# Converting the second layer's weight pieces behind the cosine passes of the first layer's second half

## The chip, the cores and the metric

One core of one Trainium2 chip runs the whole program in one launch. The metric is the device time of one execution in microseconds (us), less is better.

## The reference, cut to what matters

The program is an attention with a memory term, followed by two dense layers. Each layer has 2304 tokens, a model width of 512 and an inner width of 2048.

```python
def _moe_ref(x, w_in, w_out):
    h = x @ w_in
    g = h * np.cos(h)
    return g @ w_out

def _moe2_ref(x, w_in, w_out):
    h = x @ w_in
    sp = np.where(h > 20.0, h, np.log1p(np.exp(np.minimum(h, 20.0))))
    g = h * np.tanh(sp)
    return g @ w_out

x = attention(q, k, v, M_prev, z_prev, beta)     # 2304 x 512
return _moe2_ref(_moe_ref(x, w1_in, w1_out), w2_in, w2_out)
```

## The kernel before, in words

**Numbers.** The weights arrive in double precision, as pairs of 32-bit words. A *piece* is 128 x 512 such numbers (512 KB). It is loaded into one of two staging buffers `wst` (L123, issued by SP) and turned into single precision by five passes: POOL scales the high word (`L117`, written `wst<-wst`), ACT converts the low word (`L126`), DVE joins both with a shift (`L127`), takes the sign (`L128`) and puts it in (`L131`). Then the value is split into two float parts for the matrix engine: a high part `w` (`scaled("wh", ...)`, by ACT and POOL in turn, `L113` or `L117` written `w<-wst`) and the rest (`L161`, by DVE and POOL in turn). So pieces with an even number end on ACT and DVE, and those with an odd number on POOL twice. The last pass frees the staging buffer, into which the piece after the next is loaded.

**Layers.** Each layer's inner width is cut into two halves of 1024, and each half into four tiles of four pieces, so 16 pieces a half. `load_half` returns the tiles and a generator that converts one piece per step: `ga` and `gb` for the first layer's halves, `gc` and `gd` for the second layer's. The first layer's first half (`m1`) runs beside the attention, its second half (`m2`) after it over blocks of 512 tokens (four of them, and one of 256), and then comes the second layer (`m3`). While `m2` runs, `gc` converts the 16 pieces that `m3` begins with.

**One unit of m2.** A unit is 128 of the inner width for a block of 512 tokens. `first` computes `h` on PE (12 products, L429); `second` multiplies the split result `g` with the output weights into the sums `y` (12 products, L487). Units go in pairs: PE computes `h` of a pair, then `y` of the pair before. A pair of units needs, in this order, ACT `u<-h` twice (L376), DVE `u` twice (L377), one ACT sine over both units (L381), DVE's product with `h` twice (L384, here called the cosine product; it also frees the buffer of `h`), ACT `g<-u` twice (L113), and POOL `g<-u,g` twice (L401, the low part of `g`). The 36 units are 18 pairs, four pairs to a block of 512 tokens. At the end of a block `fin_full` adds `y` to a stored part sum (L518 loads it, L520 adds), splits it (ACT L521, POOL L524, four of each) and stores both parts (L522, L525). SP loads the next block's `x` (L474, four loads), of which two wait until the block's last `h` has been read.

**Order.** The program is recorded in the order of the code, and a scheduler then sets each engine's own order, which the engine follows strictly. `tc.issue_after(i)` is a rule for that scheduler alone: what is recorded inside it on the engine of `i` comes behind `i` on that engine. It adds no semaphore. `marks` and `last_sin` hold such instructions. Each engine's queue is in order, so an instruction that waits holds up all behind it, on SP's queue of transfers too.

Of the kernel before, what the change touches and what calls it, by code (L numbers as in the profile page):

```python
# [14 lines left out]
ALU = mybir.AluOpType  # L15
# [28 lines left out]
def attention_moe_moe_kernel(  # L44
# [14 lines left out]
    nc = tc.nc  # L59
# [84 lines left out]
    def load_half(pool, tagp, source, kind):  # L144
        tiles = []
        for tl in range(NTL):
            tiles.append([pool.tile([P, NC, SM // 2] if k < 2 else [P, 2, DM], F32R, tag=f"{tagp}{k}{tl}", bufs=1,
                                    name=f"{tagp}{k}{tl}") for k in range(4)])

        def gen():  # L150
            for tl in range(NTL):
                for n, t in enumerate(source(tl)):
                    k = n // 2 * 2
                    dH, dL = tiles[tl][k], tiles[tl][k + 1]
                    if k == 0:
                        c = 2 * n
                        dH, dL = (x[:, c:c + 2, :].rearrange("p c f -> p (c f)") for x in (dH, dL))
                    else:
                        dH, dL = (x[:, n - 2, :] for x in (dH, dL))
                    scaled("wh", dH, t)  # L160
                    turn_of(kind).tensor_tensor(dL, t, dH.bitcast(F32), ALU.subtract)  # L161
                    yield 0
        return tiles, gen()

    def from_double(win, wout, half):
        def f(tl):
            for src in weight_pieces(win, wout, half, tl):
                yield to_f32(src)
        return f

    def drain(g):
        for _ in g:
            pass
# [190 lines left out]
    last_sin = [None]  # L364
    marks = {}

    def elem_cos(cast):

        state = []

        def f(h, last):
            if not state:
                state.append(wk.tile([P, 2, SM], F32, tag="u", name="u", bufs=BUFS["u"]))
            u2 = state[0]
            u = u2[:, len(state) - 1]
            nc.scalar.activation(u.bitcast(I32), h, AF.Copy, scale=INV2PI, bias=0.25)  # L376
            nc.vector.scalar_tensor_tensor(u, u.bitcast(I32), -TWO_PI, h, ALU.mult, ALU.add)  # L377
            state.append(h)
            if len(state) < 3:
                return []  # L380
            last_sin[0] = nc.scalar.activation(u2, u2, AF.Sin, bias=c_hpi).ins  # L381
            out = []
            for i in range(2):
                nc.vector.tensor_tensor(u2[:, i], state[1 + i], u2[:, i], ALU.mult)  # L384
                out.append(split(u2[:, i], cast, "gl"))
            state.clear()
            return out
        return f
# [8 lines left out]
    def split(g, cast, kind):  # L397
        gg = wk.tile([P, 2, SM], F32R, tag="g", name="g", bufs=BUFS["g"])
        gH, gL = gg[:, 0], gg[:, 1]
        scaled(cast, gH, g)  # L400
        turn_of(kind).tensor_tensor(gL, g, gH.bitcast(F32), ALU.subtract)  # L401
        return gH, gL
# [191 lines left out]
    w_c, gc = load_half(w0p, "w2", from_double(w2i, w2o, 0), "w2l")  # L594
    m2 = ffn(b_pools, seq2, {1: w_b}, elem_cos("bh"), load_block(xsH, xsL, True), mm2_t, fin_full)
    with tc.issue_after(marks["sp"]):
        for i, _ in enumerate(m2):
            if i % 4 == 1:
                next(gc, None)
    drain(gc)  # L600
    w_d, gd = load_half(w1p, "w3", from_double(w2i, w2o, 1), "w3l")
    with tc.issue_after(last_sin[0]):
# [72 lines left out]
```

## Time and profile before

| what | value |
|---|---|
| three timed runs | 1094.81, 1095.95 and 1102.28 us, median 1095.95 us |
| the profiled execution, its own time | 1098.41 us |
| its span, first to last instruction | 1096.6 us |
| PE busy with products | 1056.2 us (96% of the span) |
| DVE, ACT, POOL busy | 517.7, 472.7, 428.4 us |
| mean granted clock of PE | 0.978 of full |

PE is TensorE, DVE VectorE, ACT ScalarE, POOL GpSimd, SP SyncE. The profile shows one execution, in us from the first instruction on. "Idle before it, ended by" names what an engine waited for last. What lies outside of the span (1098.41 less 1096.6) belongs to no instruction.

### The profile page before, as it was taken

To read this page: it belongs to the slowest core of one execution; us is meant where nothing else is said; L and a number is where in the kernel's file an instruction comes from. 1 tells how busy PE (TensorE), PEld (TensorE's weight loads), DVE (VectorE), ACT (ScalarE), POOL (GpSimd) and SP (SyncE) were. 2 spreads that over 40 slices of the span, in tenths; PEclk is the share of its full clock that TensorE was granted. 3 is DMA by queue.
4 is the path that set the end of the run, shared out by engine and by line. 5 is a ranking of instruction groups with operands and counts; after the bars stand their busy time and mean duration, and the time that the engine had idled before them with its cause. 6 is when DMAs were issued, how large, how long until landed. Compare 5 with 4: busy or idle time off the path is not lost.

```text
span 1096.6 us, 17569 instructions
## 1 busy us (share of the span) xinstructions
PE 1056.2 (96%) x6672; PEld 903.1 (82%) x6672; DVE 517.7 (47%) x1246; ACT 472.7 (43%) x947; POOL 428.4 (39%) x454
## 2 busy tenths in 40 slices
PE   6889899999999999999999999999999999999998
PEld 4767688888888899987777888988888888888897
DVE  7999885647474657655785232656200000000000
ACT  6776475637373633334454343543421222232231
POOL 5987563425242424455576333454211101010100
PEclk8998799999999999999999999999999999999999
DMA  6565442414131265333455432643300210110010
GB/s 214 184 193 189 141 145 66 140 59 138 60 95 35 80 221 182 122 114 125 165 200 183 144 116 77 218 139 97 129 6 1 77 39 0 58 39 1 20 39 20
DMA packets 66373, 117.04 MB, mean 107 GB/s; under 512 B 5616, under 2 KB 25072, under 8 KB 66288
## 3 DMA queue, kind: packets, MB, share of 16 engines
q1 hardware_dynamic: 66288, 115.91, 32.1%
q8 instruction: 53, 0.87, 0.3%
q14 instruction: 32, 0.26, 0.1%
HBM read 87.58 MB, written 28.31 MB: 106 GB/s over the span
## 4 chain that ended last, share of the span: by engine, by line
PE 70%; DVE 11%; DMA 7%; ACT 5%; POOL 4%; issue 3%; SPq 0%; ACTq 0%; POOLq 0%; DVEq 0%
PE h L429 29%; PE y L496 18%; PE y L487 12%; PE o L333 3%; PE tp L306 3%; PE sp L246 3%; DMA wst<-in_w1i_dram 2%; DVE wst L127 2%; DMA wst<-in_w1o_dram 2%; DVE wst L131 2%; DMA wst<-in_w2o_dram 1%; PE o L322 1%; DVE wst L128 1%; DMA wst<-in_w2i_dram 1%; DVE w L161 1%
## 5 line engine op out<-in xcount | busy, mean ns | idle before, releaser
L429 PE MATMUL h<-xbH,w 128*128 128x256 f32 (+1 forms) x1536 | 398.0, 340 | 8.0 <-DVE u L384 5.2
L429 PEld LDWEIGHTS h<-xbH,w 128*128 128x128 f32 x1536 | 268.1, 190 | 43.7 <-DVE u L384 6.9
L429 PE MATMUL h<-xbL,w 128*128 128x256 f32 (+1 forms) x768 | 259.3, 338 | 0.2 <-DMA xbL<-xsL 0.2
L487 PE MATMUL y<-g,w 128*128 128x256 f32 (+1 forms) x1344 | 224.8, 321 | 2.1 <-POOL g L401 1.2
L487 PEld LDWEIGHTS y<-g,w 128*128 128x128 f32 x1344 | 195.8, 195 | 24.3 <-issue 3.3
L496 PE MATMUL y<-w,g 128*128 128x512 f32 x864 | 201.8, 389 | 0.0
L496 PEld LDWEIGHTS y<-w,g 128*128 128x128 f32 x864 | 162.0, 188 | 33.4
L401 DVE TENSOR_TENSOR g<-e,g 128x512 fp32r<-128x512 f32 x36 | 25.3, 702 | 288.9 <-ACT g L113 258.3
L429 PEld LDWEIGHTS h<-xbL,w 128*128 128x128 f32 x768 | 146.1, 190 | 15.9 <-DMA xbL<-xsL 0.8
L401 POOL TENSOR_TENSOR g<-e,g 128x512 fp32r<-128x512 f32 x36 | 47.7, 1325 | 276.4 <-ACT g L113 276.4
L401 POOL TENSOR_TENSOR g<-u,g 128x512 fp32r<-128x512 f32 x72 | 95.9, 1347 | 122.0 <-ACT g L113 64.7
L274 POOL TENSOR_SCALAR at<-at,sm,omg 128x128 f32<-128x128 f32 (+2 forms) x144 | 108.4, 762 | 87.7 <-DVE sm L272 60.7
L393 ACT ACTIVATE e<-h 128x512 f32<-128x512 f32 x72 | 42.8, 594 | 216.6 <-PE h L429 216.2
L126 ACT ACTIVATE wst<-wst,c_seven 128x512 int32<-128x512 uint32 x64 | 49.3, 772 | 96.5 <-DMA wst<-in_w2o_dram 32.2
L127 DVE SCALAR_TENSOR_TENSOR wst<-wst 128x512 int32<-128x512 int32 x64 | 54.2, 847 | 68.1 <-POOL wst L117 34.4
L251 ACT ACTIVATE at<-at,mn 128x128 f32<-128x128 f32 (+3 forms) x128 | 71.0, 555 | 32.1 <-DVE mn L248 29.7
L377 DVE SCALAR_TENSOR_TENSOR u<-u,h 128x512 f32<-128x512 int32 x72 | 49.0, 682 | 61.7 <-ACT u L376 61.7
L376 ACT ACTIVATE u<-h 128x512 int32<-128x512 f32 x72 | 41.8, 591 | 80.9 <-PE h L429 72.3
L306 PE MATMUL tp<-ident,at 128*128 128x128 f32 x384 | 67.2, 294 | 8.0 <-DVE xL L338 3.1
L117 POOL TENSOR_SCALAR wst<-wst 128x512 f32<-128x512 f32 x64 | 46.9, 733 | 71.1 <-DMA wst<-in_w2o_dram 18.9
L333 PE MATMUL o<-aT,vt 128*64 128x128 f32 (+1 forms) x896 | 65.0, 276 | 0.0
L248 DVE CUSTOM_DVE_ANT_0 at<-sp,mask 128x128 f32<-128x128 f32 (+3 forms) x128 | 58.9, 481 | 10.7 <-PE sp L246 9.9
(94 smaller groups left out, 1244.9 us busy)
## 6 DMA issues: line engine op xcount, KB each, us to landing
wst<-in_w1i_dram SPq DMA_DIRECT2D x16, 512.0 KB, 3.8
wst<-in_w1o_dram SPq DMA_DIRECT2D x16, 512.0 KB, 4.1
wst<-in_w2i_dram SPq DMA_DIRECT2D x16, 512.0 KB, 3.7
wst<-in_w2o_dram SPq DMA_DIRECT2D x16, 512.0 KB, 3.6
qd<-in_qT_dram SPq DMA_DIRECT2D x16, 320.0 KB, 3.3
vt<-in_vn_dram SPq DMA_DIRECT2D x16, 320.0 KB, 3.3
xbH<-xsH SPq DMA_DIRECT2D x20, 256.0 KB, 4.7
xbL<-xsL SPq DMA_DIRECT2D x20, 256.0 KB, 4.7
```

Source lines behind the costliest of these rows:

```text
L126: nc.scalar.activation(lo, lo.bitcast(U32), AF.Relu, scale=-(2.0 ** -29), bias=c_seven)
L127: nc.vector.scalar_tensor_tensor(lo, hi, 3, lo, ALU.logical_shift_left, ALU.bitwise_or)
L248: nc.vector.tensor_tensor_reduce(at[:, :N], sp[:, :N], mask[:, SM - q0:SM - q0 + N], SSC, 3.0e38, ALU.add, ALU.min, mn[:, j:j + 1])
L251: marks["act"] = nc.scalar.activation(at[:, :N], at[:, :N], AF.Exp, bias=mn[:, j:j + 1], scale=-1.0, accum_out=sm[:, j:j + 1]).ins
L274: turn_of("sc", b == 0).tensor_scalar(at[:, :N], at[:, :N], sm[:, j:j + 1], gates[j], ALU.mult, ALU.mult)
L306: nc.tensor.transpose(tp[:, c:c + P], at[:, c:c + P], ident)
L333: marks["pe"] = nc.tensor.matmul(o[j * D:(j + 1) * D, :n], st["vt"][:kk, c, j * D:(j + 1) * D], a, start=False, stop=c == i, skip_group_ch ...
L377: nc.vector.scalar_tensor_tensor(u, u.bitcast(I32), -TWO_PI, h, ALU.mult, ALU.add)
L401: turn_of(kind).tensor_tensor(gL, g, gH.bitcast(F32), ALU.subtract)
L429: nc.tensor.matmul(h[:, a * T:(a + 1) * T], w_[:, c, f0:f0 + P], x_[c], start=m == 0, stop=m == 3 * NC - 1)
L487: nc.tensor.matmul(y[e // per][:, cols], w_[:, f, es], g_, start=fst and m == 0 and e % per == 0, stop=lst and m == 2, skip_group_check=True)
L496: nc.tensor.matmul(y[t], g_[:, tsl], w_[:, f, :], start=fst and m == 0, stop=lst and m == 2, skip_group_check=True)
```

## The change

The two cosine products of a pair are now remembered as `marks["cos"]` (the second of them stays), and each step of `gc` in `m2` is recorded inside two `issue_after` blocks: on DVE the piece's passes come behind the last cosine product recorded so far, on ACT behind the last sine recorded so far. A step of `gc` is still taken once per pair of units, right after the pair before has got its `second`; POOL and SP get no such rule.

```diff
@@ -381,7 +381,7 @@
             for i in range(2):
-                nc.vector.tensor_tensor(u2[:, i], state[1 + i], u2[:, i], ALU.mult)
+                marks["cos"] = nc.vector.tensor_tensor(u2[:, i], state[1 + i], u2[:, i], ALU.mult).ins
                 out.append(split(u2[:, i], cast, "gl"))
@@ -596,7 +596,8 @@
     with tc.issue_after(marks["sp"]):
         for i, _ in enumerate(m2):
             if i % 4 == 1:
-                next(gc, None)
+                with tc.issue_after(marks["cos"]), tc.issue_after(last_sin[0]):
+                    next(gc, None)
     drain(gc)
```

What that does to the order shows at three places. On ACT, at the second pair of `m2`, the order before was this (`wst` is a staging buffer, `w_6519` the high part of the third piece):

```order
L126 ACTIVATE wst<-wst,c_seven 128x512
L376 ACTIVATE u<-h 128x512
L126 ACTIVATE wst<-wst,c_seven 128x512
L376 ACTIVATE u<-h 128x512
L381 ACTIVATE u<-u,c_hpi 128x1024
L113 ACTIVATE w_6519<-wst 128x512
L113 ACTIVATE g<-u 128x512 x2
```

and now, for the second and the third pair, it is this:

```order
L376 ACTIVATE u<-h 128x512 x2
L381 ACTIVATE u<-u,c_hpi 128x1024
L126 ACTIVATE wst<-wst,c_seven 128x512
L113 ACTIVATE g<-u 128x512 x2
L376 ACTIVATE u<-h 128x512 x2
L381 ACTIVATE u<-u,c_hpi 128x1024
L126 ACTIVATE wst<-wst,c_seven 128x512
L113 ACTIVATE g<-u 128x512 x2
L113 ACTIVATE w_6519<-wst 128x512
```

Two conversions stood before the pair's sine, one of them between the two `u<-h`; now one stands behind each sine and none before it. DVE's passes moved in the same way, behind L384.

On POOL, about the end of the first block of `m2`, the order before was this:

```order
L401 TENSOR_TENSOR g<-u,g 128x512
L117 TENSOR_SCALAR wst<-wst 128x512
L401 TENSOR_TENSOR g<-u,g 128x512
L524 TENSOR_TENSOR yl<-yp,yh 128x512 x2
L117 TENSOR_SCALAR wst<-wst 128x512
L117 TENSOR_SCALAR w_6525<-wst 128x512
L161 TENSOR_TENSOR w_6526<-wst,w_6525 128x512
L524 TENSOR_TENSOR yl<-yp,yh 128x512 x2
```

and now it is this, from the pair ahead of the block's end to the pair behind it:

```order
L401 TENSOR_TENSOR g<-u,g 128x512 x2
L117 TENSOR_SCALAR w_6519<-wst 128x512
L161 TENSOR_TENSOR w_6520<-wst,w_6519 128x512
L117 TENSOR_SCALAR wst<-wst 128x512
L401 TENSOR_TENSOR g<-u,g 128x512 x2
L524 TENSOR_TENSOR yl<-yp,yh 128x512 x3
L117 TENSOR_SCALAR wst<-wst 128x512
L524 TENSOR_TENSOR yl<-yp,yh 128x512
L401 TENSOR_TENSOR g<-u,g 128x512 x2
```

One piece's first pass stands between each two pairs of L401; where it follows an L161, that L161 frees the very buffer into which its piece is loaded.

On SP, the loads of `x` for the third block of `m2` stood before behind four loads of pieces:

```order
L518 DMA yp<-ysP 128x512
L123 DMA wst<-in_w2i_dram 128x2x512 x2
L123 DMA wst<-in_w2o_dram 128x1024 x2
L474 DMA xbH<-xsH 128x2x512
L474 DMA xbL<-xsL 128x2x512 x2
L474 DMA xbH<-xsH 128x2x512
```

and now behind two:

```order
L525 DMA ysL<-yl 128x512
L123 DMA wst<-in_w2o_dram 128x1024
L123 DMA wst<-in_w2i_dram 128x2x512
L474 DMA xbL<-xsL 128x2x512
L474 DMA xbH<-xsH 128x2x512
L474 DMA xbL<-xsL 128x2x512
L474 DMA xbH<-xsH 128x2x512
L123 DMA wst<-in_w2i_dram 128x2x512
```

The last piece load ahead of `x` now takes the buffer of a piece of two pairs earlier. On PE nothing moves but six products of `y`, at one place.

## Rows read from the trace of the kernel before

**Rows 1.** Stages: length, busy PE, PEld, DVE, ACT, POOL, clock, DMA share, GB/s
```profile
520.00:540.00 20.00, 17.72 (x72) 14.17 (x71) 13.23 (x20) 9.23 (x15) 11.47 (x10) 0.91 0.59 209
...
620.00:640.00 20.00, 20.00 (x90) 16.56 (x89) 7.12 (x11) 8.23 (x12) 5.09 (x5) 1.00 0.26 91
```

**Rows 2.** Waits of PE's products, 470 to 800 us: total, times, longest, us
```profile
PE h L429 <- DVE u L384: 5.2, 4, 2.3
PE h L429 <- DMA xbH<-xsH: 2.0, 1, 2.0
```

**Rows 3.** Timeline of PE: start us, us, instruction, idle before it and releaser
```profile
507.66 0.39 PE L429 MATMUL h<-xbH,w 128*128 128x512 f32 x1
...
511.98 0.50 PE L429 MATMUL h<-xbH,w 128*128 128x512 f32 x1 [1.44 <-DVE u L384]
...
525.47 0.50 PE L429 MATMUL h<-xbH,w 128*128 128x512 f32 x1 [2.28 <-DVE u L384]
...
585.39 0.50 PE L429 MATMUL h<-xbH,w 128*128 128x512 f32 x1 [2.00 <-DMA xbH<-xsH]
...
595.14 0.39 PE L429 MATMUL h<-xbH,w 128*128 128x512 f32 x1
```

**Rows 4.** Timeline of ACT at the second pair
```profile
506.93 0.77 ACT L126 ACTIVATE wst<-wst,c_seven 128x512 int32<-128x512 uint32 x1 [2.10 <-DMA wst<-in_w2o_dram]
507.61 0.57 ACT L376 ACTIVATE u<-h 128x512 int32<-128x512 f32 x1
510.05 1.15 ACT L381 ACTIVATE u<-u,c_hpi 128x1024 f32<-128x1024 f32 x1 [1.87 <-DVE u L377]
```

**Rows 5.** Timeline of DVE at the second pair
```profile
509.33 0.68 DVE L377 SCALAR_TENSOR_TENSOR u<-u,h 128x512 f32<-128x512 int32 x1
...
511.23 1.29 DVE L384 TENSOR_TENSOR u<-h,u 128x512 f32<-128x512 f32 x2 [0.61 <-ACT u L381]
```

**Rows 6.** The chain that ended last, pieces in time: start us, us, what
```profile
611.62 5.44 PE y L487 x24
...
622.50 5.44 PE y L487 x24
...
694.20 4.79 PE h L429 x21
```

**Rows 7.** Timeline of ACT, a pair without conversions
```profile
613.01 1.15 ACT L381 ACTIVATE u<-u,c_hpi 128x1024 f32<-128x1024 f32 x1 [0.76 <-DVE u L377]
614.92 1.23 ACT L113 ACTIVATE g<-u 128x512 fp32r<-128x512 f32 x2 [0.76 <-DVE u L384]
```

**Rows 8.** Timeline of DVE, the same pair
```profile
614.20 1.29 DVE L384 TENSOR_TENSOR u<-h,u 128x512 f32<-128x512 f32 x2 [1.22 <-ACT u L381]
```

**Rows 9.** Timeline of POOL, the same pair, and a pass of a block's end
```profile
615.63 2.53 POOL L401 TENSOR_TENSOR g<-u,g 128x512 fp32r<-128x512 f32 x2 [5.14 <-ACT g L113]
...
639.95 1.31 POOL L524 TENSOR_TENSOR yl<-yp,yh 128x512 fp32r<-128x512 f32 x1
```

**Rows 10.** Tile wst, 500 to 600 us: ns min/median/max, first and last start
```profile
L117 POOL TENSOR_SCALAR wst<-wst x17: 638/650/1197, 503.7 to 596.6; 128x512 f32<-128x512 f32 x17
L126 ACT ACTIVATE wst<-wst,c_seven x15: 751/767/802, 503.6 to 584.2; 128x512 int32<-128x512 uint32 x15
L127 DVE SCALAR_TENSOR_TENSOR wst<-wst x15: 685/694/1679, 504.4 to 585.0; 128x512 int32<-128x512 int32 x15
L128 DVE TENSOR_SCALAR wst<-wst x15: 416/425/1514, 505.6 to 586.2; 128x512 int32<-128x512 int32 x15
L131 DVE TENSOR_TENSOR wst<-wst x15: 685/687/1672, 508.4 to 587.8; 128x512 int32<-128x512 int32 x15
...
L161 DVE TENSOR_TENSOR w<-wst,w x8: 674/684/1715, 500.2 to 585.6; 128x512 fp32r<-128x512 f32 x8
...
L161 POOL TENSOR_TENSOR w<-wst,w x8: 1291/1314/1761, 510.0 to 591.4; 128x512 fp32r<-128x512 f32 x8
...
DMA to landing us min/median/max: 3.5/3.7/5.9
```

## The prediction

> **What bounds the kernel now.** I read the table of stages first, then what PE waited for, then the timelines of the four engines about the waits. PE is the bound nearly everywhere: from 620 to 640 us it is busy for 20.00 of 20 us at full clock [rows 1]. In the second half of the first layer there is one stretch where it isn't, from 500 to 600 us, as in the stage from 520 to 540 us with 17.72 us at 0.91 of the clock [rows 1]. PE waits there four times for the cosine product L384 (5.2 us in all) and once for a load of x (2.0 us) [rows 2].
>
> The size of that loss is read from PE's own pitch. A pair of units, 24 products of h and 24 of y, takes 622.50 - 611.62 = 10.88 us where nothing disturbs [rows 6]. From the third pair's h at 507.66 us to the tenth's at 595.14 us there are seven pairs [rows 3]: 87.48 us, where 7 x 10.88 = 76.16 would do. So 11.3 us are lost there: the waits of rows 2 (7.2 us), short waits for g, the slow products after the longest wait (the stage mean of 0.91 is a stretch at the lower of the clock's two levels, 1.2 instead of 2.4 GHz, and it comes after the 2.28 us gap), and the slow start after each gap.
>
> Why the waits arise shows at the second pair. ACT stands at a piece's L126, waits 2.10 us for its load until 506.93 us, and only then runs the pair's second u<-h at 507.61 [rows 4]. On DVE the piece's passes come next, and the second L377 starts at 509.33, the cosine product at 511.23 [rows 5]; PE's second h of the third pair needs the buffer that this product frees and goes on at 511.98 us, 1.44 us late [rows 3]. So the chain of a pair is held up by piece passes that wait for transfers and stand ahead of it in the same queues. The load of x at 585.39 us is late for the same reason: SP issued it behind four piece loads, each of which waits for a staging buffer.
>
> **The change part by part.** No instruction is added or removed. The same 16 pieces are converted, one per pair instead of two or so, and behind the sine and the cosine product instead of ahead.
>
> *The chain of a pair.* Take T as the end of a pair's h, 611.62 us in the undisturbed pair [rows 6]. The sine runs from T+1.4 to T+2.5, L384 from T+2.6 to T+3.9, g from T+3.3, and L401 from T+4.0 to T+6.5 [rows 7 to 9]. The needs are later. The next pair's second h wants the first product of L384 (T+3.3) after y (5.44) and one h (2.72), at T+8.2: 4.9 us to spare. The pair's own y wants the first L401, 1.3 us long, at T+10.9: it may start as late as T+9.6, 5.6 us to spare. These margins now cover the passes of a piece.
>
> *ACT.* L126 (0.77) stands between the sine and g. The sine ends at T+2.5, so L126 ends at T+3.3, just when g could start anyway: cost nothing. If its cover (L384 on DVE) were gone, it would cost 0.77 us out of 5.6.
>
> *DVE.* L127, L128 and L131 (0.69 + 0.43 + 0.69 = 1.8 us) follow L384 and end at T+5.7; for an even piece ACT's high part (as long as L126, 0.77 at most) and L161 (0.68) follow until T+7.2 [rows 10]. The next L377 is due only after T+8.2. Cost nothing, by one us of cover.
>
> *POOL, where a wait is added.* Behind L401 an odd piece has its high part and L161, 0.65 + 1.31 us, until T+8.5. Only then is its buffer free; the load takes 3.7 us (median) to 5.9 (longest) [rows 10], so it is there at T+12.2 to T+14.4, and L117 ends at T+12.9 to T+15.1. The next pair's L401 is queued behind that L117 and is due at T+10.9+4.0 = T+14.9. So it is 0.2 us late at the most, with 5.6 us to spare behind it. I take nothing.
>
> *SP.* The last piece load ahead of x now waits for the buffer of an even piece, free at T+7.2 of its pair, while the x loads wait for the next pair's h to end, at T+10.9. The x wait of 2.0 us should go.
>
> *The end.* Piece 15 goes with the sixteenth pair. Counted on from the tenth pair at 595.14 us by 10.88 us, that pair's h ends at about 666 us, less what is saved, and its last pass some 9 us later. The second layer's first h comes at 694.20 us [rows 6]: nearly 20 us of cover, and none of its waits rest on the last pieces.
>
> *Passes that meet.* The same DVE passes range from 0.69 to 1.68 (L127), 0.43 to 1.51 (L128) and 0.69 to 1.67 us (L131) [rows 10]. The Trainium skill (SBUF — State Buffer, section Who interferes with whom) says that a DVE instruction with two SBUF inputs, or in a two-port mode, and a GpSimd instruction that reads SBUF take one shared port pair, and that the loser is blocked for the whole instruction. It speaks against this change, which sets the DVE passes right beside L401 in every pair; the long ends of the rows agree with it. By the medians the sum stays as it is; by that rule the time would be that of the first rival below.
>
> *Sum.* All of the 11.3 us may go; below nothing they can't be had again, since no other stall lies in this half. Bounds: 11.3 us gained, or, if the block ends keep a loss, down to 4 or 5 gained. I take 10.3, with 1.0 us left for three block ends at about 0.3 each, near the undisturbed end because the block ends that ran without pieces (after 620 us) show no wait of PE. The profiled execution would go from 1098.41 to 1088.1 us (its span from 1096.6 to 1086.3). The timed median, 1095.95, lies 2.5 us below the profiled time; the same gain puts it at 1085.7 us.
>
> **The rivals.** *Block ends keep a loss.* There four passes L524 (1.31 each) join POOL, and L117 of a piece stands between the third and the fourth, ahead of the next pair's L401. With the longest DVE passes everywhere, L384's end at T+3.9 plus 1.68 + 1.51 + 1.67 + 0.77 + 1.72 puts the buffer free at T+11.3, the load in at T+17.2, L117 and one L524 done at T+19.2 [rows 9, 10]; the next L401 must start by T+20.5. That is 1.3 us to spare, and a load held up by 3 us behind the stores of that block end would cost 1.7 us, three times: some 5 us, 1091 us. For it: the long rows, and four stores in the same queue. Against: by the medians 7.6 us are to spare.
>
> *Nothing moves in time.* The waits come from the block ends and the load of x rather than from queue order, and turn up elsewhere: about 1096 us. For it: half of the loss is not in the four L384 waits. Against: the pairs without pieces run at 10.88 us, block ends included.
>
> *The other side: POOL stands in front of its own load.* Each L117 waits for a load that can't start before the L161 ahead of it. T+8.5 + load + 0.65 passes T+20.5 from a load of 11.3 us on; from there each us of load is a us of PE in up to 14 pairs. At 12.1 us the gain is eaten; at 12.4 us 15 us are lost and the time is 1101 us; at 12.8 us it is over 1107. For it: x loads, part sums and stores share the transfer engines with the pieces. Against: the longest landing of 17 was 5.9 us, in a stretch with 209 GB/s [rows 1, 10].
>
> **How the numbers follow.** Chances: forecast 0.70, block ends 0.16, nothing 0.07, POOL 0.07. A measurement of this kernel tells about 1%, here 11.0 us, from no change, and the most that can be gained is 11.3. So the forecast itself lies at the border: I put 0.36 of its 0.70 beyond 1% and 0.34 within. With 0.16, 0.07 and 0.03 of POOL's within 1%, that is 0.60 the same; 0.04 slower. The range goes from 1083.5 (all 11.3 gained, and a run as far below the median as the fastest of the three, 1.1 us) to 1093.5 (the block ends at half as much again); it leaves out "nothing", POOL and a little below.
>
> **What would show it.** Right: PE at 20.00 of 20 us in all stages from about 500 us on, no wait of h for L384 over half a us, the tenth pair's h near 584 us, the clock at 1.00 throughout, the second layer's first h near 683 us, L126 spread over all of this half, about one per 10.88 us. Wrong in a step: waits of y for L401 (POOL's queue), of h for a load of x (SP's), or of h for L384 every fourth pair (block ends). The forecast is wrong as a whole if the seven pairs from the third to the tenth take more than 82 us, or if a loss of over 3 us comes up outside of them.

## The result and the profile after

| | before | after |
|---|---|---|
| timed runs, median | 1095.62 us of 4 (1094.81 to 1102.28) | 1084.97 us of 4 (1079.77 to 1091.44) |
| ratio, 95% interval | | 0.9891 [0.9861, 0.992] |
| profiled execution, its span | 1098.41, 1096.6 us | 1085.15, 1083.4 us |
| mean granted clock of PE | 0.978 | 0.987 |

The changed kernel is 1.1% faster: 10.65 us between the medians, where 10.3 was forecast (1085.7 us, measured 1084.97). The interval alone allows gains from 8.8 to 15.2 us, and the four timed runs of after lie up to 11.7 us apart, so that the medians came within 0.7 us of the forecast is partly luck; what follows rests on the traces.

A stage of after that answers to [rows 1] (length, busy PE, PEld, DVE, ACT, POOL, clock, DMA share, GB/s):

```profile
520.00:540.00 20.00, 20.00 (x90) 16.57 (x89) 12.06 (x16) 9.28 (x14) 9.51 (x10) 1.00 0.47 164
```

All stages from 500 to 760 us have PE at 20.00 of 20 us and a clock of 1.00. What PE's products waited for from 470 to 800 us in after (total, times, longest, us). The one line that is left is the end of the half before, and it stands in before too, with 0.9 us:

```profile
PE y L487 <- DVE g L115: 1.0, 1, 1.0
```

Both lines of [rows 2] are gone, and PE is full at full clock. The chain that ended last shows it as PE's pitch (start us, us, what):

```profile
505.88 5.44 PE h L429 x24
511.32 5.44 PE y L487 x24
...
582.03 5.44 PE h L429 x24
...
680.93 4.79 PE h L429 x21
```

From the third pair's h at 505.88 us to the tenth's at 582.03 are 76.15 us, 7 x 10.88, where before took 87.48 us [rows 3].

**Where the 13.2 us of span went.** To compare runs I read one stretch in each timeline of PE: from the last 46 products y of the half before to the first product of the second layer's y, L496. First before's two ends, then after's:

```profile
491.37 5.77 PE L487 MATMUL y<-g,w 128*128 128x256 f32 x46
...
710.73 4.47 PE L496 MATMUL y<-w,g 128*128 128x512 f32 x19
```

```profile
489.42 5.77 PE L487 MATMUL y<-g,w 128*128 128x256 f32 x46
...
697.46 4.70 PE L496 MATMUL y<-w,g 128*128 128x512 f32 x20
```

That is 219.36 us before and 208.04 after: 11.32 us, all that the prediction said could be had. Another 1.95 us lie ahead of the stretch, where the change does nothing; they can't be counted as its gain, since two runs below with one and the same order of instructions (cut256 and cut128) began the stretch 5.6 us apart, at 492.09 and 486.54 us. The expectations quoted below use a stretch inside this one, 33 us shorter (175.05 us in after, 186.54 in before); 33 is to be added to their numbers.

**A pair in after.** Take T as the end of its h, 511.32 us. First ACT and then DVE (start us, us, instruction, idle before it and its releaser):

```profile
512.71 1.15 ACT L381 ACTIVATE u<-u,c_hpi 128x1024 f32<-128x1024 f32 x1 [0.76 <-DVE u L377]
513.76 0.75 ACT L126 ACTIVATE wst<-wst,c_seven 128x512 int32<-128x512 uint32 x1
514.62 1.23 ACT L113 ACTIVATE g<-u 128x512 fp32r<-128x512 f32 x2
```

```profile
513.89 1.29 DVE L384 TENSOR_TENSOR u<-h,u 128x512 f32<-128x512 f32 x2 [1.22 <-ACT u L381]
515.10 0.68 DVE L127 SCALAR_TENSOR_TENSOR wst<-wst 128x512 int32<-128x512 int32 x1
...
518.17 0.97 DVE L161 TENSOR_TENSOR w<-wst,w 128x512 fp32r<-128x512 f32 x1 [0.74 <-ACT w L113]
```

L126 waits for nothing, where it waited 2.10 us in [rows 4], and the sine and the cosine product start at T+1.4 and T+2.6 as in a pair without a piece [rows 7, 8]. In before, ACT waited for 13 loads from 500 to 600 us (total, times, longest):

```profile
ACT wst L126 <- DMA wst<-in_w2o_dram: 14.9, 8, 3.7
ACT wst L126 <- DMA wst<-in_w2i_dram: 9.2, 5, 3.3
```

In after no L126 of these pieces waits for its load. POOL still does; its waits in after from 490 to 680 us:

```profile
POOL wst L117 <- DMA wst<-in_w2i_dram: 31.9, 8, 5.1
POOL wst L117 <- DMA wst<-in_w2o_dram: 23.6, 6, 5.2
```

So the waits for loads did not vanish. The 24.1 us on ACT are gone, and POOL's, 15.8 us in before's 500 to 600 us, are now 55.5; but POOL has them to spare, and none reaches PE.

### The profile page after: what moved, and what is told of

Same layout as the page of the kernel before. It is cut to its first block, busy times and chain, and to the rows that moved or that the text cites. A ratio compares the mean times of both kernels' runs of the same rounds, so it can differ in the third digit from the quotient of the medians.

```text
span 1083.4 us, 17564 instructions
## 1 busy us (share of the span) xinstructions
PE 1051.3 (97%) x6672; PEld 901.1 (83%) x6672; DVE 531.2 (49%) x1246; ACT 474.2 (44%) x947; POOL 434.3 (40%) x454
## 4 chain that ended last, share of the span: by engine, by line
PE 80%; DVE 7%; ACT 5%; DMA 4%; issue 2%; POOL 1%; SPq 0%; ACTq 0%; POOLq 0%; DVEq 0%
PE h L429 33%; PE y L496 18%; PE y L487 16%; PE o L333 3%; PE tp L306 3%; PE sp L246 3%; DMA wst<-in_w1i_dram 1%; DMA wst<-in_w1o_dram 1%; PE mp L286 1%; PE o L322 1%; DVE wst L131 1%; ACT at L251 1%; DVE wst L127 1%; DVE w L161 1%; DVE at L248 1%
## 5 line engine op out<-in xcount | busy, mean ns | idle before, releaser
L496 PE MATMUL y<-w,g 128*128 128x512 f32 x864 | 201.8, 389 | 0.0
L496 PEld LDWEIGHTS y<-w,g 128*128 128x128 f32 x864 | 161.9, 188 | 33.5
L401 DVE TENSOR_TENSOR g<-e,g 128x512 fp32r<-128x512 f32 x36 | 25.3, 702 | 288.9 <-ACT g L113 258.4
L401 POOL TENSOR_TENSOR g<-e,g 128x512 fp32r<-128x512 f32 x36 | 47.6, 1322 | 275.6 <-ACT g L113 275.6
L401 POOL TENSOR_TENSOR g<-u,g 128x512 fp32r<-128x512 f32 x72 | 102.3, 1438 | 70.7 <-DVE g L115 51.7
L117 POOL TENSOR_SCALAR wst<-wst 128x512 f32<-128x512 f32 x64 | 45.6, 713 | 116.7 <-DMA wst<-in_w2i_dram 40.6
L376 ACT ACTIVATE u<-h 128x512 int32<-128x512 f32 x72 | 42.3, 594 | 97.0 <-PE h L429 85.8
L126 ACT ACTIVATE wst<-wst,c_seven 128x512 int32<-128x512 uint32 x64 | 48.9, 766 | 68.6 <-DMA wst<-in_w1o_dram 19.6
L377 DVE SCALAR_TENSOR_TENSOR u<-u,h 128x512 f32<-128x512 int32 x72 | 49.0, 683 | 51.0 <-ACT u L376 50.8
L127 DVE SCALAR_TENSOR_TENSOR wst<-wst 128x512 int32<-128x512 int32 x64 | 50.0, 781 | 41.6 <-ACT wst L126 20.4
L131 DVE TENSOR_TENSOR wst<-wst 128x512 int32<-128x512 int32 x64 | 68.4, 1070 | 1.1
```

The source lines that it names most:

```text
L126: nc.scalar.activation(lo, lo.bitcast(U32), AF.Relu, scale=-(2.0 ** -29), bias=c_seven)
L127: nc.vector.scalar_tensor_tensor(lo, hi, 3, lo, ALU.logical_shift_left, ALU.bitwise_or)
L131: nc.vector.tensor_tensor(dst, lo, hi, ALU.bitwise_xor)
L496: nc.tensor.matmul(y[t], g_[:, tsl], w_[:, f, :], start=fst and m == 0, stop=lst and m == 2, skip_group_check=True)
```

## The experiments

All of them change where or how fast the second half's 16 pieces are converted, or their loads. The table gives the stretch of each and what it loses against after's 208.04 us.

| run | pieces in a pair, and where | stretch, us | loss, us |
|---|---|---|---|
| before | two or so, ahead of the pair's chain | 219.36 | 11.32 |
| after | one, behind sine and cosine product | 208.04 | |
| sine_only | one, the same order as after | 208.04 | 0.0 |
| own_ahead | one, L126 ahead of its pair's sine | 208.03 | 0.0 |
| mid_chain | one, ahead of sine and cosine product | 208.61 | 0.6 |
| cos_only | one, L126 a pair ahead of its piece's place | 243.71 | 35.7 |
| three_in_two | three in two pairs, behind | 218.96 | 10.9 |
| two_a_pair | two, behind | 220.23 | 12.2 |
| two_mid | two, ahead of sine and cosine product | 219.88 | 11.8 |
| two_no_loads | two, behind, no loads | 208.58 | 0.5 |
| before_no_loads | up to three, ahead, no loads | 223.27 | 15.2 |
| cut256, cut128 | as after, slower loads | 208.03, 208.03 | 0.0 |
| cut64 | as after, still slower loads | 212.64 | 4.6 |

In all runs but sine_only and own_ahead the scheduler also moved some of PE's products past each other, and in the two without loads much of the order earlier in the program too; the stretch holds the same products in all. The kernel before was timed anew beside each group of runs, at 1097.09 (one run) to 1100.29 us in the median, so the ratios and the stretches can be compared across groups, and the times can't.

### Each of the two rules alone

```diff
# sine_only
-                with tc.issue_after(marks["cos"]), tc.issue_after(last_sin[0]):
+                with tc.issue_after(last_sin[0]):
# cos_only
-                with tc.issue_after(marks["cos"]), tc.issue_after(last_sin[0]):
+                with tc.issue_after(marks["cos"]):
```

> Only the rule behind the sine is kept, the one behind the cosine product is taken out. The scheduler then makes the same order on every engine as with both rules, so this is a repeat of the changed kernel. The measure in all these runs is the stretch on PE from the third pair's first h of the first layer's second half to the second layer's first h: 186.5 us before, 175.05 us after, and 16 pairs without a wait can't be shorter. Expected: 175.0 to 175.4 us, ratio to the kernel before 0.986 to 0.992. If the gain of the first comparison was chance or came from elsewhere, the stretch is 178 us or more.

> Only the rule behind the cosine product is kept. On DVE the passes stay behind L384; on ACT the conversion L126 moves ahead of the sine in most pairs, one piece per pair as in the changed kernel. Theory (what costs is a pass that waits for its load in front of the pair's chain; here the load has landed some 7 us earlier, so L126 costs its own 0.75 us out of 4.9 to spare): stretch 175.0 to 176.0 us, no wait of h for L384 over 0.5 us. Rival (a pass ahead of the sine costs by its place): 178 us or more, with waits of h for L384.

Measured: sine_only 208.04 us in the stretch, 1086.35 us timed, ratio 0.9869 [0.9844, 0.9893]; cos_only 243.71 us, 1122.33 us timed, ratio 1.0183 [1.0139, 1.0226]. sine_only has the order of after on every engine, so the rule on DVE adds nothing. Without the rule on ACT the kernel is slower than before, where I expected next to no loss. A pair of cos_only on ACT, then the issue of the load in question on SP:

```profile
523.36 0.76 ACT L126 ACTIVATE wst<-wst,c_seven 128x512 int32<-128x512 uint32 x1 [6.50 <-DMA wst<-in_w2o_dram]
524.02 1.13 ACT L381 ACTIVATE u<-u,c_hpi 128x1024 f32<-128x1024 f32 x1
```

```profile
519.64 0.33 SPq L123 DMA_DIRECT2D wst<-in_w2o_dram  x1
```

The piece whose L126 stands ahead of the sine here is not the pair's own but the next one's. Its load was issued only at 519.64 us, when the buffer came free, and landed 3.7 us later, not some 7 us before it was needed, as I had expected; the sine stood behind it for all of that. In the whole half PE then waits as follows, from 490 to 710 us:

```profile
PE h L429 <- DMA xbH<-xsH: 11.1, 4, 3.3
PE h L429 <- DVE u L384: 7.7, 7, 1.9
```

The larger part is for x: its loads stand on SP behind a piece load that has to wait for its buffer, and the first of them goes out at 532.13 us, 39.6 us after the start of the stretch (492.51 us), against 30.2 us in after.

### The place: ahead of the sine, or in mid-chain

If standing ahead of the sine is what hurts, a pair's own piece there must hurt as well. own_ahead puts L126 directly ahead of its pair's sine and leaves the order of PE, DVE and POOL as in after; mid_chain puts the whole piece behind the pair's first u<-h and first L377, so ahead of sine and cosine product.

```diff
# own_ahead (marks["u"] is the last u<-h, L376, of a pair)
+                with tc.issue_after(marks["cos"]), tc.issue_after(marks["u"]):
# mid_chain (u0 and v0 are a pair's first L376 and first L377)
+                with tc.issue_after(marks["v0"]), tc.issue_after(marks["u0"]):
```

> ACT's rule is tied to the pair's last u<-h instead of to its sine: L126 of each piece now stands directly ahead of its pair's sine, and is the pair's own piece (one per pair, its load issued a pair earlier); PE, DVE and POOL have the order of after. Stretch from the third pair's first h of m2 to the second layer's first h, 175.0 us in after. Theory (the loss of cos_only came from L126 standing one pair ahead of its own, so that it waited for a load that had just been issued, and not from standing ahead of the sine): the 0.77 us of L126 fits into the 4.9 us that the next h leaves, so 175.0 to 175.7 us, and the timed ratio within 0.3% of after's. Rival (any L126 ahead of the sine delays the chain, so the place behind the sine is what pays): at least 3 us more, 178 us or above.

> Pace of the changed kernel, place of the kernel before: each piece goes behind the pair's first u<-h and first L377, so that L126 stands between the two u<-h and L127, L128, L131 (and in even pieces L161) between the two L377 and the cosine product. Theory (waiting for loads is what costs, at one piece a pair the load is long there): the chain gets 1 to 2.5 us longer out of 4.9 to spare, stretch 175.0 to 176.5 us. Rival (the place in the chain is what costs): the waits of h for L384 come back, stretch 179 to 187 us.

Measured: own_ahead 208.03 us, timed 1086.44, ratio 0.9882 [0.9852, 0.9912]; mid_chain 208.61 us, timed 1090.16, ratio 0.9898 [0.9871, 0.9926]. Neither place costs more than 0.6 us. ACT in own_ahead shows why:

```profile
516.69 0.60 ACT L376 ACTIVATE u<-h 128x512 int32<-128x512 f32 x1 [2.06 <-PE h L429]
517.18 0.77 ACT L126 ACTIVATE wst<-wst,c_seven 128x512 int32<-128x512 uint32 x1
518.04 1.15 ACT L381 ACTIVATE u<-u,c_hpi 128x1024 f32<-128x1024 f32 x1
```

The sine starts 1.35 us after the last L376, as in after (511.35 to 512.71 us): L126 fills the 0.76 us in which ACT waits for L377 anyway, because its load is in already.

### The pace

```diff
# two_a_pair, under after's two rules
-                    next(gc, None)
+                    next(gc, None); next(gc, None)
# three_in_two, under after's two rules
+                    next(gc, None); i % 8 == 1 and next(gc, None)
# two_mid: mid_chain's rules, and
+                    next(gc, None); next(gc, None)
```

> Place of the changed kernel, about the pace of the kernel before: two pieces behind each pair's sine and cosine product, so that all 16 are done within eight pairs and both staging buffers come free only at a pair's end. Theory (passes that wait for a load hold up what is queued behind them): the loads land 4 to 5 us into the next pair, second conversions stand in front of g and L401 and use up most of 5.6 us to spare: 175.5 to 180 us, with waits of y for POOL or ACT rather than of h for L384. Rival (place alone counts): 175.0 to 175.4 us. Rival (pace alone counts): 184 us or more.

> Under both rules of after, two pieces in every second pair and one in the others (three in two pairs). Stretch as above, 175.0 us in after, 186.5 in before, about 187.2 with two pieces in each pair. Theory (the pace decides: a piece's load can only start when the buffer of the piece two earlier is free, and two buffers feed one piece per pair in time): the pairs with two lose a little, 177 to 184 us in all. Rival (only the place behind the cosine product counts, and two_a_pair lost by something else): 175.0 to 176 us.

> Two pieces in each pair in the place of mid_chain (behind the pair's first u<-h and first L377, so ahead of its sine and cosine product), loads as in after. With mid_chain (one a pair, +0.6 us) and two_a_pair (+12.2 us behind the cosine) it gives the four corners of place and pace. Stretch as above. If pace and place add up: about 187 to 189 us. If the place matters once the loads come late, since a pass that waits there holds up the sine and L384: 192 us or more. Should it lie below 182, the place behind the cosine would be the worse one at this pace.

Measured: 220.23 us (timed 1099.23, ratio 0.9991 [0.9962, 1.0021], so no faster than before), 218.96 us (one run of 1098.67) and 219.88 us (one run of 1103.89). At the pace of before all of the gain is gone wherever the pieces stand, and half a piece more in a pair loses 10.9 us, more than the 2 to 9 us that I expected. two_mid lies where place and pace add up, and shows no price of the place beyond the scatter of these three.

In three_in_two the load of x breaks first. Its SP (start us, us in its queue, issue), then PE:

```profile
512.48 12.46 SPq L123 DMA_DIRECT2D wst<-in_w2i_dram  x2
524.99 0.46 SPq L474 DMA_DIRECT2D xbL<-xsL  x1
525.50 0.46 SPq L474 DMA_DIRECT2D xbH<-xsH  x1
```

```profile
528.13 0.62 PE L429 MATMUL h<-xbH,w 128*128 128x512 f32 x2
...
532.53 0.61 PE L429 MATMUL h<-xbH,w 128*128 128x512 f32 x1 [2.65 <-DMA xbH<-xsH]
...
533.37 1.05 PE L429 MATMUL h<-xbH,w 128*128 128x512 f32 x2
```

Two piece loads hold SP for 12.46 us, since the second waits for a staging buffer; only then are the x loads behind them issued: 36.8 us after the start of the stretch (488.20 us), where after issues them 30.2 us after it (519.65 less 489.42). PE waits 6.2 us in three such waits, and behind the 2.65 us wait two products take 1.05 us instead of 0.62: the clock is at its lower level there (0.78 of full as the mean from 530 to 535 us). This is the x wait of [rows 2], three times over. It is not the same everywhere at this pace: of PE's waits from 490 to 690 us, x has 4.9 of 8.5 us in two_a_pair, but 1.1 of 6.6 in two_mid, whose longest wait, 2.1 us, is for ACT's part of g.

### Loads or passes

```diff
# two_no_loads is two_a_pair, and before_no_loads is before, with
+        rw = raw[0] if raw else st
+        if not raw: nc.sync.dma_start(st, src)
...
+    rt = wk.tile([P, SM, 2], I32, tag="raw", name="raw", bufs=1); nc.sync.dma_start(rt, next(weight_pieces(w2i, w2o, 0, 0))); raw.append(rt); w_c, gc = load_half(w0p, "w2", from_double(w2i, w2o, 0), "w2l")
```

> Two pieces in each pair under both rules, all of them converted from one tile that is loaded once: the weights of the second layer's first half are wrong, and the pieces' loads are left out. It tells what the 12.2 us that two_a_pair lost were. Stretch as above (two_a_pair about 187.2 us). If the loads (waits of L126 and L117 for them, and x loads queued behind them on SP) cost it: 175 to 178 us. If the passes themselves, two sets of them in a pair's time on DVE and POOL, cost it: 184 us or more.

> The kernel before, but 14 of the 16 pieces of the second layer's first half are converted from one tile that is loaded once, so these weights are wrong and their loads are left out; the same passes run on the same engines, the scheduler puts up to three pieces into a pair. Theory (the waits for loads in front of the chain are the cost): the stretch falls from 186.5 to 175 to 179 us. Rival (the passes themselves, two or three a pair ahead of the chain, are the cost): 182 us or more.

Measured: two_no_loads 208.58 us, before_no_loads 223.27 us (one run each, 1095.3 and 1107.65 us). The longest of PE's waits in two_no_loads from 490 to 690 us, and one of its stages:

```profile
PE y L487 <- DVE g L115: 0.8, 1, 0.8
...
```

```profile
520.00:540.00 20.00, 20.00 (x90) 16.57 (x89) 17.27 (x22) 10.29 (x16) 13.46 (x12) 1.00 0.00 0
```

So 11.65 of the 12.2 us that two_a_pair lost go with the loads; two sets of passes in a pair fit beside the chain. DVE is then busy for 17.27 of 20 us, against 6.43 from 620 to 640 us in this run, where no piece is left. By that, and as an estimate, a pair of 10.88 us has 3.5 us of DVE work of its own and 2.95 for each piece: two make 9.4 us, three 12.3, more than the pair lasts.

That is where my expectation of before_no_loads failed: without loads to wait for, nine L126 of this half stand in the time of three pairs, from 493.9 to 531 us. A stage of this run, and PE's waits:

```profile
500.00:520.00 20.00, 17.81 (x78) 14.27 (x77) 18.59 (x27) 11.42 (x17) 14.59 (x14) 0.91 0.25 79
```

```profile
PE y L487 <- POOL g L401: 4.6, 4, 1.8
PE y L487 <- ACT g L113: 3.0, 2, 2.0
```

DVE is busy 18.59 of 20 us, and PE waits for g instead of for L384 or x. It loses 15.2 us for another reason than before does, and does not tell how much of before's own loss is due to its loads; two_no_loads tells that for two pieces a pair only.

### Slower loads

```diff
# cut256, cut128, cut64 (j = 64, 32, 16): these pieces are read in runs of 256, 128, 64 bytes
+        wc = win.bitcast(I32).rearrange("(c p) (i q j) -> p c q i j", p=P, q=4, j=64)
...
+            yield wc[:, c // 2, tl] if cut else wi[:, c:c + 2, f0:f0 + 2 * P, :]
```

> The changed kernel with slower loads: the pieces of the second layer's first half are read in runs of 256 bytes instead of 2 or 4 KB (other weights of the same array, so these weights are wrong, the same bytes). Margins as in the prediction: PE waits only where a load takes over 11.3 us. Expected load 5 to 8 us, stretch 175.0 to 175.6 us. Rival (POOL in front of its own load costs from the start): each us of load over 3.7 shows in 14 pairs, 190 us or more.

> As before with runs of 128 bytes. Expected load 8 to 13 us, near the limit of 11.3 us: 175 to 185 us; where the median load is below 10 us, 175.0 to 176.5 us. The first waits should be of y for POOL's L401, or of h for x behind the piece loads on SP. Rival (POOL costs from the start): over 200 us.

> As before with runs of 64 bytes. Expected load 14 to 25 us, beyond the limit: PE waits in nearly every pair, and the stretch is set by the cycle of the two staging buffers; at a load of 18 us about 6 us lost in each of 14 pairs, 230 to 270 us. If no wait of PE comes up although the median load is over 13 us, the limit of 11.3 us is wrong.

Loads as slow as I expected did not come about. From 490 to 680 us they landed after 3.9 / 4.6 / 5.4 us (shortest, median, longest) in cut256, 3.7 / 5.2 / 6.1 in cut128 and 3.6 / 7.0 / 9.2 in cut64. The first two lose nothing (one run each, 1087.9 and 1082.94 us). cut64 (1090.17 us) loses 4.6, though its longest load is below the 11.3 us from which the prediction let POOL decide. SP, POOL and PE at its first loss:

```profile
503.15 0.55 SPq L123 DMA_DIRECT2D wst<-in_w2i_dram  x1
```

```profile
511.18 0.65 POOL L117 TENSOR_SCALAR wst<-wst 128x512 f32<-128x512 f32 x1 [6.45 <-DMA wst<-in_w2i_dram]
511.79 2.53 POOL L401 TENSOR_TENSOR g<-u,g 128x512 fp32r<-128x512 f32 x2
```

```profile
499.83 5.60 PE L487 MATMUL y<-g,w 128*128 128x512 f32 x24
513.11 5.55 PE L487 MATMUL y<-g,w 128*128 128x512 f32 x23 [2.01 <-POOL g L401]
```

At this pair, the second of the half, T is 499.83 us, and its L401 is due at T+9.6 = 509.4. The load in front of it is issued at 503.15 only, so it may take 509.4 - 0.65 - 503.15 = 5.6 us. It took 8.0, and L401 came 2.4 us late, 2.0 of them seen by PE. The next pair's y loses 1.7 us in the same way, and the waits for L401 are 3.7 of the 4.6 us. This is the mechanism of the third rival, at a lower limit.

## Why the prediction was right, and where its steps were off

- **The loss and its place.** 87.48 - 76.16 = 11.3 us to be had between the third and the tenth pair: after takes 76.15 us there, and 11.32 us are gone from the whole stretch. The tenth pair's h was forecast near 584 us and the second layer's first h near 683; they came at 582.03 and 680.93, both 2 us early, by the 1.95 us that lie ahead of the stretch.
- **The mis-sized term of the sum.** 1.0 us was kept for three block ends; it measured nothing. With the 1.95 us ahead of the stretch, which no step foresaw, the profiled execution came to 1085.15 us, where 1088.1 was forecast. At the first block end, T = 533.08 us, the worst case put the next L401 at T+19.2, due at T+20.5. It started at T+17.6, with one L524 between the piece's L117 and it, as POOL shows:

```profile
548.19 1.11 POOL L117 TENSOR_SCALAR wst<-wst 128x512 f32<-128x512 f32 x1 [3.17 <-DVE u L384]
549.27 1.46 POOL L524 TENSOR_TENSOR yl<-yp,yh 128x512 fp32r<-128x512 f32 x1
550.68 2.98 POOL L401 TENSOR_TENSOR g<-u,g 128x512 fp32r<-128x512 f32 x2
```

- **ACT and DVE at nothing.** Right for ACT: L126 ended at T+3.2 (forecast T+3.3). Right for DVE in what it cost PE, but the passes were mis-sized. From 490 to 670 us in after they took (ns, shortest/median/longest):

```profile
L127 DVE SCALAR_TENSOR_TENSOR wst<-wst x17: 683/683/1114, 491.9 to 656.5; 128x512 int32<-128x512 int32 x17
L128 DVE TENSOR_SCALAR wst<-wst x17: 427/912/1405, 493.1 to 657.3; 128x512 int32<-128x512 int32 x17
L131 DVE TENSOR_TENSOR wst<-wst x17: 693/1658/1668, 493.5 to 658.7; 128x512 int32<-128x512 int32 x17
```

  Their medians add up to 3.3 us instead of 1.8 [rows 10]. The rule that the prediction cited from the Trainium skill (SBUF — State Buffer, section Who interferes with whom) had it right that the passes meet L401 on POOL; in mid_chain, where they stand elsewhere, L131's median is 694 ns. The loss of the first rival, which the prediction tied to that rule, did not come. The one us of cover named for DVE held in the pair shown above: its last pass ended at T+7.8, and the next L377 started at T+8.9 (520.20 us). It did not hold at the second pair (T = 500.44 us, behind a first pair that was itself late) and at the block ends, where three of the four L520, which the sum for DVE left out, stand among the passes. DVE at both places:

```profile
501.80 0.69 DVE L161 TENSOR_TENSOR w<-wst,w 128x512 fp32r<-128x512 f32 x1 [0.73 <-ACT w L113]
502.40 1.28 DVE L377 SCALAR_TENSOR_TENSOR u<-u,h 128x512 f32<-128x512 int32 x2
504.90 1.29 DVE L384 TENSOR_TENSOR u<-h,u 128x512 f32<-128x512 f32 x2 [1.22 <-ACT u L381]
...
542.67 0.96 DVE L161 TENSOR_TENSOR w<-wst,w 128x512 fp32r<-128x512 f32 x1 [0.74 <-ACT w L113]
543.56 0.68 DVE L377 SCALAR_TENSOR_TENSOR u<-u,h 128x512 f32<-128x512 int32 x1
```

  At the second pair both L377 come behind the piece's last pass, and L384 at T+4.5 instead of T+2.6. At the first block end (T = 533.08 us) the last pass ends at T+10.5, and the L377 behind it is 1.6 us late. What spared PE there was not the cover but the 4.9 us that the next h leaves behind L384.
- **SP.** Right: the last piece load ahead of x went out at 519.17 us, T+7.9 of the third pair (forecast T+7.2), and the loads of x right behind it.
- **POOL.** That L117 waits in front of L401 and has room for it was right. Behind an undelayed pair the forecast holds: the next L401 was forecast at T+14.9, and behind the pair of T = 522.20 us it started at 537.09, T+14.9. The step "until T+8.5" was not right: there POOL's L161 ended at 531.93, T+9.7, since the longer DVE passes come ahead of it:

```profile
530.61 1.32 POOL L161 TENSOR_TENSOR w<-wst,w 128x512 fp32r<-128x512 f32 x1
535.58 0.66 POOL L117 TENSOR_SCALAR wst<-wst 128x512 f32<-128x512 f32 x1 [3.66 <-DMA wst<-in_w2i_dram]
537.09 2.86 POOL L401 TENSOR_TENSOR g<-u,g 128x512 fp32r<-128x512 f32 x2 [0.85 <-ACT g L113]
```

  And "0.2 us late at the most" was too small. At the second pair L401 starts at T+6.9, and at the third (516.86 us) at T+5.5, instead of T+4.0, each behind an L117 that waits for its load; that takes up to 2.9 of the 5.6 us to spare:

```profile
506.76 0.64 POOL L117 TENSOR_SCALAR wst<-wst 128x512 f32<-128x512 f32 x1 [5.19 <-DMA wst<-in_w2o_dram]
507.37 3.17 POOL L401 TENSOR_TENSOR g<-u,g 128x512 fp32r<-128x512 f32 x2
```

  The limit for a load is thus 20.5 - 9.7 - 0.65 = 10.1 us behind an undelayed pair; behind the second pair, whose L161 on POOL ends at T+12.1 (512.55 us), 7.7 us; and at the second pair itself, whose L117 stands ahead of that same pair's L401, 5.6 us as worked out above. The rival was nearer than its 11.3 us let it seem, with loads that took 5.1 us at the longest in after. No load of any run with one piece in a pair took 10.1 us, so the first of these limits was not tested. (The rival's "over 1107" at a load of 12.8 us is 1085.7 + 14 x 1.5 = 1106.7; nothing hangs on it.)
- **The reason.** The prediction gave two things as one: the pieces go to one in a pair, and they go behind the chain. The runs separate them. One in a pair loses 0.0 to 0.6 us in each of three places, as long as it is the pair's own piece; with the next pair's piece ahead of the sine (cos_only) it loses 35.7. Two in a pair lose 11.8 and 12.2 us in two, as much as before in its own. The gain comes from the pace and from the load that is in a pair ahead; the place behind the cosine product, which the diff names, is worth 0.6 us at the most. The code takes one step of `gc` in a pair in before too; what the rules add is that the scheduler can no longer run ahead of that; with the rule on DVE alone (cos_only), ACT still does, by one piece. That a pass which waits for its load holds up the chain was right, and cos_only shows it at its worst. Which part of before's 11.32 us came from L384, and which from x and the slow products behind both, was not taken apart; nor was, for two in a pair, the part of the passes' own loads and that of the x loads behind them.

## What to carry to other kernels

Where a side job shares in-order queues with the chain that feeds the bottleneck, count buffers and loads first: with two staging buffers, one piece in a pair's time had its load in before ACT and DVE came to it (but for two waits of at most 0.9 us on ACT in mid_chain), while POOL, which could wait, did wait; then the place in the queues hardly mattered (0.0 to 0.6 us); half a piece more cost 10.9 us. Tie each piece to an instruction that comes once in a period, and see that what stands at that spot is the piece whose load is already in, not the next one. Look at the issuing queue too: a load that waits for a buffer holds up every load behind it, whatever that one is for.

## What the runs showed of the hardware that was not expected

Loads read in runs of 256 and 128 bytes landed at a median of 4.6 and 5.2 us, against 3.7 in after, and in runs of 64 bytes at 7.0: far less than I had expected of cutting them up. An L131 of 0.69 us took 1.66 us as a rule where it met L401 on POOL; L401 itself grew less, from a mean of 1354 ns in before to 1532 in after (490 to 670 us), and in mid_chain, where the passes stand elsewhere, its mean is 1290 ns. And a wait of 2.65 us at PE cost more than itself: two products of 0.62 us took 1.05 behind it.
